# Sums written in place in PSUM, input sums in smaller pieces, and a tile of weights loaded sooner: one core, attention and four experts

## The chip, the cores and the metric

The kernel runs on one core of one Trainium2 chip. Times are microseconds (us) of device time. PE is TensorE, DVE VectorE, ACT ScalarE, POOL GpSimd, SP SyncE.

## The reference

q, k and v (2 batches, 8 heads, 576 positions, 64 columns, float32) are rotated and go through softmax attention. The result, 1152 tokens of 512 columns, goes through four experts, all of them for every token, mixed by weights p:

```python
p = domain_probs / (domain_probs.sum(-1, keepdims=True) + 1e-09)
for e in range(E):                       # E = 4
    h = np.maximum(x @ w1[e], 0.0)       # w1[e]: 512 x 1024
    out += p[:, e:e + 1] * (h @ w2[e])   # w2[e]: 1024 x 512
```

## The kernel before, in words

**High and low halves.** A float32 matrix is held as a high half, rounded to the type that TensorE multiplies (float32r), and a low half, the rest. A product is three matmuls: high by high, high by low, low by high. The split is a copy on ScalarE (`wh`, `hH`, `tH`, ...) and a subtraction on VectorE or GpSimd (`wl`, `hL`, `tL`, ...). Line 142 is the subtraction in the helper `split`; it serves weights, inputs and their sums.

**Chunks.** The tokens go in two chunks. Chunk zero has 512 of batch 0, chunk one the other 640. Attention of batch 0 runs first. Attention of batch 1 runs beside the experts of chunk zero (tiles `ph`, `hH`, `hL`, `po`, lines 557 to 606). Then chunk one runs alone, its four experts one after another: a first layer (products `p`, lines 716 to 718) and a second layer (`po`, lines 796 to 798).

**Chunk one's first layer.** A block of 256 of the 1024 hidden columns is a 2 x 2 block product over two halves of the 512 input columns and two halves of the 640 tokens. It is done with seven block products instead of eight, p1 to p7, from sums of weight blocks (`sf`, split into `sh` and `sl`) and sums of input blocks (class Quarters: `s0` to `s3`, split into `t1H`, `t1L`, `tH`, `tL`). Expert 0 does p1 and p2 of all four blocks first, eight products, then five a block; experts 1 to 3 do seven a block. Each product has 128 partitions x 320 columns and takes one of the eight PSUM banks in turn. VectorE combines the results: `u` = p6 + p1, `v` = p7 + u, `u` = p5 + u; and the four results of a block, `c`, are p5 + v, p2 + p1, p4 + v, p3 + u (line 746, each into an SBUF tile). ScalarE takes relu of `c` as the high half `hH` (line 755), VectorE takes max(c, 0) - hH as the low half `hL` (line 757). The low half is issued one product later, so that it stands behind the next result's add in VectorE's queue.

**Weights.** A tile of 512 KB is loaded by SyncE into one of two raw buffers, copied by ScalarE (`wh`) and subtracted by GpSimd (`wl`), or summed by VectorE first (`sf`). `wts.next()` loads one tile and splits the one before. A raw buffer is free when the last reader of the tile before the last is done; the ring of split tiles has five.

**Order.** The program keeps the order in which it is written. A heap of (time, function) pairs, `plan`, sets that order up to the end of chunk zero: times are positions in the plan, not microseconds, and one step of the experts is one unit. `quarter_step` runs the sums' generators a piece at a time; a `yield` ends a piece. Each engine then runs its own queue in that order, and waits where a semaphore is not yet set.

**The end of chunk zero.** The last pair's attention ends with `tmp` (ScalarE), `xf` (VectorE), 20 matmuls of the tail rows (line 416), a division (line 403), the high half `xH` (line 406) and the low half `xL` (line 409, GpSimd). The last input sums need them. Then VectorE mixes the four `po` of chunk zero's last expert into `acc` (line 606), which frees their banks, and SyncE stores `acc`. In the first layer's class, the bank counter of chunk one starts at 4.

Of the kernel before, what the change touches and what calls it, by code (L numbers as in the profile page):

```python
# [16 lines left out]
AF = mybir.ActivationFunctionType  # L17
# [38 lines left out]
def kernel(  # L56
# [88 lines left out]
    class Pair:  # L145
# [262 lines left out]
        def out_low(self):  # L408
            nc.gpsimd.tensor_tensor(out=self.dst[1], in0=self.xf, in1=f32(self.dst[0]), op=ALU.subtract)

# [112 lines left out]
    class Moe:  # L523
# [18 lines left out]
        def expert(self, e):  # L542
# [24 lines left out]
            for f in range(NF):  # L567
                fb, fi = divmod(f, FB)
                wH, wL = (w[:, fi, :] for w in wts.got[c, e, 1, fb])
                for t in range(n // P):  # L570
                    sH, sL = (x[:, t * P : (t + 1) * P] for x in hh[f])
                    nc.tensor.matmul(po[t], lhsT=sH, rhs=wH, start=(f == 0), stop=False)  # L572
                    nc.tensor.matmul(po[t], lhsT=sH, rhs=wL, start=False, stop=False)  # L573
                    nc.tensor.matmul(po[t], lhsT=sL, rhs=wH, start=False, stop=(f == NF - 1))  # L574
                    if f == NF - 1:
                        self.mix(e, t, po[t])
                if fi == FB - 1:
                    if e == E - 1 and f == NF - 1:
                        wts.load()
                    else:  # L580
                        wts.next()
                yield
# [36 lines left out]
    class Quarters:  # L619
# [25 lines left out]

        def split(self, eng, name, i, j):
            hi, lo = ((y[:, j] for y in self.t1) if i == 0 else (y[:, i - 1, j] for y in self.t))
            split(nc.scalar, eng, self.at[name], hi, lo)

        def first(self, eng, j):  # L650

            self.whole(eng, "s0", j, 0, 1)
            self.whole(eng, "s1", j, 0, 0)
            yield True
            self.less(eng, "s0", ("s1", "s1"))
            self.split(eng, "s1", 0, j)
            yield True

        def second(self, eng, j):

            self.whole(eng, "s2", j, 1, 1)
            self.less(eng, "s2", ("s0", "s0"))
            self.split(eng, "s0", 2, j)
            yield True
            self.less(eng, "s2", ("s2", "s1"))
            self.split(eng, "s2", 1, j)
            yield True
            self.whole(eng, "s3", j, 1, 0)
            self.less(eng, "s3", ("s3", "s2"))
            self.split(eng, "s3", 3, j)  # L670
            yield True
# [9 lines left out]
    class Moe1(Moe):  # L681
# [7 lines left out]
        def __init__(self, ctx, quarters):  # L689
# [6 lines left out]
            ]  # L696
            self.used = 4
            self.x, self.lows = {}, []
# [6 lines left out]
        def product(self, e, i, p):  # L705
# [21 lines left out]
            elif p == "p7":  # L727
                x["v", i] = self.temp("v", e, i)
                self.add(x["v", i], o, x["u", i])
            elif p == "p5":  # L730
                self.hidden(e, 2 * i + 1, 1, o, x["v", i])
                self.add(x["u", i], o, x["u", i])
            elif p == "p2":
# [14 lines left out]
        def hidden(self, e, f, t, o, other):  # L748

            if f not in self.hh:  # L750
                self.hh[f] = [self.h.tile([P, self.n], F32R, tag=f"h{x}{f}", name=f"h{x}1_{e}_{f}") for x in "HL"]
            hi, lo = (x[:, t * TH : (t + 1) * TH] for x in self.hh[f])
            c = self.temp("c", e, f"{f}{t}", 4)
            self.add(c, o, other)
            nc.scalar.activation(out=hi, in_=c, func=AF.Relu)  # L755
            self.lows.append(
                lambda: nc.vector.scalar_tensor_tensor(  # L757
                    out=lo, in0=c, scalar=0.0, in1=f32(hi), op0=ALU.max, op1=ALU.subtract
                )
# [273 lines left out]
    plan.at(end + last - NF + 0.1, start_quarters)  # L1033
    for i in range(7):
        plan.at(end + last - NF + 0.2 + 0.75 * i, quarter_step)
    for i in range(3):
        plan.at(end + last - 1.3 + 0.01 * i, quarter_step)
# [55 lines left out]
```

## Time and profile before

| | us |
|---|---|
| median of 3 runs | 608.73 (608.7 to 613.69) |
| the profiled execution | 611.2, span 609.4 |
| chunk one begins | 373.8 in the span |
| busy TensorE (matmul) | 554.0, 91% |
| busy VectorE, ScalarE, GpSimd | 372.3, 281.2, 332.6 |

The span runs from the first to the last instruction; the time of the profiled execution has 1.8 us around it. The share of a whole run says little here, since chunk one has other limits than attention: waits and stretches of chunk one are what to read.

### The profile page before, as it was taken

How to read it: one execution, taken by the hardware profiler on the slowest of the kernel's cores; microseconds unless marked ns; L12 is line 12 of the kernel's file. 1: busy time of each engine (PE TensorE's matmuls, PEld its weight loads, DVE VectorE, ACT ScalarE, POOL GpSimd, SP SyncE). 2: the span in 40 equal slices, each digit the busy share in tenths (PEclk: the TensorE clock that was granted, in tenths of full speed). 3: DMA queues.
4: the chain of work that ended last, by engine and by line, in shares of the span. 5: the costliest groups of instructions: out<-in, count | busy, mean ns of one | idle time of the engine just before them, and what ended most of it. 6: DMA issues, size and time to landing. Idle time of an engine off the chain costs nothing.

```text
span 609.4 us, 8591 instructions
## 1 busy us (share of the span) xinstructions
PE 554.0 (91%) x3229; PEld 481.6 (79%) x3229; DVE 372.3 (61%) x595; ACT 281.2 (46%) x545; POOL 332.6 (55%) x223
## 2 busy tenths in 40 slices
PE   3788888899999999999999977968998999999896
PEld 2678777778888888888888856957897898789785
DVE  6786898334363435343354335797889788868822
ACT  4677777355444545455355532453243333324310
POOL 7849992257824873485353772364753673466300
PEclk9998999899999999999999998999999999999999
DMA  5053131064124123422332213332232123123102
GB/s 157 7 152 100 36 96 57 1 177 143 69 79 143 57 86 88 130 69 70 96 103 70 70 34 113 94 115 93 71 104 69 38 88 117 35 69 104 35 1 86
DMA packets 42459, 50.67 MB, mean 83 GB/s; under 512 B 7218, under 2 KB 32050, under 8 KB 42418
## 3 DMA queue, kind: packets, MB, share of 16 engines
q1 hardware_dynamic: 41618, 49.38, 27.2%
q10 hardware_dynamic: 800, 0.75, 0.4%
q8 instruction: 25, 0.41, 0.3%
q14 instruction: 16, 0.13, 0.1%
HBM read 43.34 MB, written 2.36 MB: 75 GB/s over the span
## 4 chain that ended last, share of the span: by engine, by line
PE 51%; DVE 17%; POOL 10%; issue 9%; ACT 8%; DMA 5%; SPq 0%; DVEq 0%; POOLq 0%; ACTq 0%
PE sc L282 5%; PE ph L596 4%; POOL wl L142 4%; PE ph L598 4%; PE ph L597 4%; PE po L574 4%; DMA wr<-in_moe_w_dram 4%; PE po L572 4%; PE po L573 4%; PE pp L315 3%; PE po L796 3%; PE po L797 3%; PE po L798 3%; ACT wh L135 3%; POOL sl L142 2%
## 5 line engine op out<-in xcount | busy, mean ns | idle before, releaser
L142 POOL TENSOR_TENSOR wl<-wr,wh 128x1024 fp32r<-128x1024 f32 x64 | 155.4, 2429 | 139.0 <-ACT wh L135 138.9
L135 ACT ACTIVATE wh<-wr 128x1024 fp32r<-128x1024 f32 x64 | 67.4, 1052 | 34.4 <-PE po L574 16.0
L293 DVE TENSOR_REDUCE mx<-sc 128x1 f32<-128x576 f32 x72 | 54.1, 753 | 36.8 <-PE sc L282 36.2
L757 DVE SCALAR_TENSOR_TENSOR hL<-c,hH 128x320 fp32r<-128x320 f32 x64 | 65.7, 1026 | 11.7 <-ACT hH L755 11.6
L142 POOL TENSOR_TENSOR sl<-sf,sh 128x1024 fp32r<-128x1024 f32 x16 | 38.4, 2400 | 62.0 <-ACT sh L135 56.7
L796 PE MATMUL po<-wh,hH 128*128 128x512 f32 x160 | 63.4, 396 | 7.1 <-DVE u L746 4.2
L301 ACT ACTIVATE e<-sc,mx 128x576 f32<-128x576 f32 x72 | 53.2, 740 | 27.7 <-DVE mx L293 27.1
L797 PE MATMUL po<-wl,hH 128*128 128x512 f32 x160 | 62.4, 390 | 0.0
L798 PE MATMUL po<-wh,hL 128*128 128x512 f32 x160 | 62.3, 390 | 0.0
L558 DVE SCALAR_TENSOR_TENSOR hL<-ph,hH 128x512 fp32r<-128x512 f32 x32 | 22.1, 692 | 61.7 <-ACT hH L557 61.7
L755 ACT ACTIVATE hH<-c 128x320 fp32r<-128x320 f32 x64 | 29.8, 468 | 61.8 <-DVE c L746 61.8
L315 PE MATMUL pp<-ident,e 128*128 128x128 f32 x288 | 46.0, 284 | 8.4 <-DVE e L387 5.3
L572 PE MATMUL po<-wh,hH 128*128 128x512 f32 x128 | 52.3, 409 | 0.0
L596 PE MATMUL ph<-xH,wh 128*128 128x512 f32 x128 | 51.5, 402 | 0.0
L336 DVE TENSOR_TENSOR ptL<-pp,ptH 128x512 fp32r<-128x512 f32 x64 | 43.9, 686 | 11.4 <-ACT ptH L332 10.9
L574 PE MATMUL po<-wh,hL 128*128 128x512 f32 x128 | 50.2, 393 | 0.0
L598 PE MATMUL ph<-xH,wl 128*128 128x512 f32 x128 | 50.1, 392 | 0.0
L512 DVE TENSOR_TENSOR sf<-wr 128x256 f32<-128x256 f32 x32 | 38.9, 1255 | 18.3 <-DMA wr<-in_moe_w_dram 18.3
L597 PE MATMUL ph<-xL,wh 128*128 128x512 f32 x128 | 50.0, 391 | 0.0
L573 PE MATMUL po<-wl,hH 128*128 128x512 f32 x128 | 50.0, 391 | 0.0
L332 ACT ACTIVATE ptH<-pp 128x512 fp32r<-128x512 f32 x64 | 38.1, 595 | 25.7 <-PE x L365 17.3
L315 PEld LDWEIGHTS pp<-ident,e 128*128 128x128 f32 x288 | 35.1, 145 | 15.3 <-issue 3.9
(162 smaller groups left out, 1370.6 us busy)
## 6 DMA issues: line engine op xcount, KB each, us to landing
wr<-in_moe_w_dram SPq DMA_DIRECT2D x68, 512.0 KB, 3.5
k2T<-kT SPq DMA_DIRECT2D x14, 288.0 KB, 4.0
rawv<-in_v_dram SPq DMA_DIRECT2D x8, 256.0 KB, 2.9
out_dram<-acc SPq DMA_DIRECT2D x8, 256.0 KB, 2.6
rawk<-in_k_dram SPq DMA_DIRECT2D x7, 256.0 KB, 4.2
rawq<-in_q_dram SPq DMA_DIRECT2D x7, 256.0 KB, 3.2
rawv<-in_v_dram SPq DMA_DIRECT2D x16, 32.0 KB, 2.6
tabs<-in_rope_dram ACTq DMA_DIRECT2D x1, 320.0 KB, 3.3
```

Source lines behind the costliest of these rows:

```text
L135: nc.scalar.activation(out=hi, in_=src, func=AF.Copy)
L142: eng_l.tensor_tensor(out=lo, in0=src, in1=f32(hi), op=ALU.subtract)
L315: nc.tensor.transpose(pp[:, c * P : (c + 1) * P], self.e[u][:, c * P : (c + 1) * P], ident)
L572: nc.tensor.matmul(po[t], lhsT=sH, rhs=wH, start=(f == 0), stop=False)
L573: nc.tensor.matmul(po[t], lhsT=sH, rhs=wL, start=False, stop=False)
L574: nc.tensor.matmul(po[t], lhsT=sL, rhs=wH, start=False, stop=(f == NF - 1))
L596: nc.tensor.matmul(o, lhsT=wH[:, kt], rhs=xh, start=(kt == 0), stop=False)
L597: nc.tensor.matmul(o, lhsT=wH[:, kt], rhs=xl, start=False, stop=False)
L598: nc.tensor.matmul(o, lhsT=wL[:, kt], rhs=xh, start=False, stop=(kt == KT1 - 1))
L796: nc.tensor.matmul(po[t], lhsT=sH, rhs=wH, start=(f == 0), stop=False)
L797: nc.tensor.matmul(po[t], lhsT=sH, rhs=wL, start=False, stop=False)
L798: nc.tensor.matmul(po[t], lhsT=sL, rhs=wH, start=False, stop=(f == NF - 1))
```

## The change

Four edits.

- **Sums in place.** `hidden` adds into the product's own PSUM bank (`o`) rather than into an SBUF tile `c`. Relu and the low half read the bank. For p5 the second sum `u` is therefore made before the add overwrites p5.
- **Input sums in pieces.** Quarters issues sums, high halves and low halves in separate pieces, and more of them are placed in the plan (nine steps 0.6 apart and six at the end, rather than seven 0.75 apart and three). For the last pair of attention the low half `xL` is made by VectorE, not GpSimd.
- **Bank counter.** It starts at 0, not 4. The pool hands out banks as the tags are first asked for: in the built program the first product of chunk one lies in bank 0 before and after, the second in bank 1, and so on.
- **Weights.** In the last expert of chunk zero, the second tile for the weight sums is loaded one step sooner, ahead of the stores of `acc` in SyncE's queue.

```diff
         def out_low(self):
-            nc.gpsimd.tensor_tensor(out=self.dst[1], in0=self.xf, in1=f32(self.dst[0]), op=ALU.subtract)
+            eng = nc.vector if (self.b, self.hp) == (B - 1, NP - 1) else nc.gpsimd
+            eng.tensor_tensor(out=self.dst[1], in0=self.xf, in1=f32(self.dst[0]), op=ALU.subtract)
...
-                if fi == FB - 1:
-                    if e == E - 1 and f == NF - 1:
-                        wts.load()
-                    else:
-                        wts.next()
+                if e == E - 1 and f == NF - 2:
+                    wts.load()
+                elif fi == FB - 1 and (e, f) != (E - 1, NF - 1):
+                    wts.next()
...
         def first(self, eng, j):
             self.whole(eng, "s0", j, 0, 1)
             self.whole(eng, "s1", j, 0, 0)
+            self.less(eng, "s0", ("s1", "s1"))
             yield True
-            self.less(eng, "s0", ("s1", "s1"))
-            self.split(eng, "s1", 0, j)
+            self.high("s1", 0, j)
             yield True
+            self.low(eng, "s1", 0, j)
         def second(self, eng, j):
             self.whole(eng, "s2", j, 1, 1)
             self.less(eng, "s2", ("s0", "s0"))
-            self.split(eng, "s0", 2, j)
+            self.less(eng, "s2", ("s2", "s1"))
             yield True
-            self.less(eng, "s2", ("s2", "s1"))
-            self.split(eng, "s2", 1, j)
+            self.high("s0", 2, j)
+            self.high("s2", 1, j)
             yield True
             self.whole(eng, "s3", j, 1, 0)
             self.less(eng, "s3", ("s3", "s2"))
-            self.split(eng, "s3", 3, j)
+            self.low(eng, "s0", 2, j)
+            self.low(eng, "s2", 1, j)
+            yield True
+            self.high("s3", 3, j)
+            yield True
+            self.low(eng, "s3", 3, j)
             yield True
...
-            self.used = 4
+            self.used = 0
...
             elif p == "p5":
+                self.add(x["u", i], o, x["u", i])
                 self.hidden(e, 2 * i + 1, 1, o, x["v", i])
-                self.add(x["u", i], o, x["u", i])
...
-            c = self.temp("c", e, f"{f}{t}", 4)
-            self.add(c, o, other)
-            nc.scalar.activation(out=hi, in_=c, func=AF.Relu)
+            self.add(o, o, other)
+            nc.scalar.activation(out=hi, in_=o, func=AF.Relu)
             self.lows.append(
                 lambda: nc.vector.scalar_tensor_tensor(
-                    out=lo, in0=c, scalar=0.0, in1=f32(hi), op0=ALU.max, op1=ALU.subtract
+                    out=lo, in0=o, scalar=0.0, in1=f32(hi), op0=ALU.max, op1=ALU.subtract
...
-    for i in range(7):
-        plan.at(end + last - NF + 0.2 + 0.75 * i, quarter_step)
-    for i in range(3):
+    for i in range(9):
+        plan.at(end + last - NF + 0.2 + 0.6 * i, quarter_step)
+    for i in range(6):
         plan.at(end + last - 1.3 + 0.01 * i, quarter_step)
```

ScalarE's queue in the last steps of chunk zero, before, from the copy of the tail's transposed exponentials (`at`) to the high halves of the last input sums:

```order
L351 ACTIVATE at_3_8_3865<-pp_3_8_3860 128x512
L135 ACTIVATE t1H<-s_3837 128x320
L372 ACTIVATE tmp_3_3_3872<-x_112 64x256
L135 ACTIVATE wh_0_0_3_3889<-wr_0_0_3_3818 128x1024
L425 ACTIVATE xH_74<-x_112 128x64
L406 ACTIVATE xH_74<-xf_3_3537 128x512
```

and now:

```order
L351 ACTIVATE at_3_8_3861<-pp_3_8_3856 128x512
L372 ACTIVATE tmp_3_3_3870<-x_112 64x256
L651 ACTIVATE t1H<-s_3866 128x320
L135 ACTIVATE wh_0_0_3_3888<-wr_0_0_3_3821 128x1024
L426 ACTIVATE xH_74<-x_112 128x64
L406 ACTIVATE xH_74<-xf_3_3537 128x512
```

`tmp`, which the last tile of attention needs, and `t1H`, the high half of an input sum that GpSimd makes, have changed places. Two high halves `tH` have moved ahead of the `tmp` before this one, too.

VectorE's queue from the last division of attention to the first mixing of chunk zero's output (`acc`), before:

```order
L403 TENSOR_TENSOR xf_3_3537<-xf_3_3537,pr_3_3903 128x512
L429 TENSOR_TENSOR xL_76<-x_112,xH_74 128x64
L639 TENSOR_TENSOR s_3925<-xH_74,xL_76 128x320
L644 TENSOR_TENSOR s_3835<-s_3925,s_3835 128x320
L142 TENSOR_TENSOR tL<-s_3835,tH 128x320
L644 TENSOR_TENSOR s_3925<-s_3925,s_3837 128x320
L142 TENSOR_TENSOR tL<-s_3925,tH 128x320
L639 TENSOR_TENSOR s_3933<-xH_74,xL_76 128x320
L644 TENSOR_TENSOR s_3933<-s_3933,s_3925 128x320
L142 TENSOR_TENSOR tL<-s_3933,tH 128x320
L606 SCALAR_TENSOR_TENSOR acc_0_1511<-po_3_0_3673,probs,acc_0_1511 128x512
```

and now:

```order
L403 TENSOR_TENSOR xf_3_3537<-xf_3_3537,pr_3_3902 128x512
L430 TENSOR_TENSOR xL_76<-x_112,xH_74 128x64
L410 TENSOR_TENSOR xL_76<-xf_3_3537,xH_74 128x512
L639 TENSOR_TENSOR s_3927<-xH_74,xL_76 128x320
L644 TENSOR_TENSOR s_3864<-s_3927,s_3864 128x320
L644 TENSOR_TENSOR s_3927<-s_3927,s_3866 128x320
L639 TENSOR_TENSOR s_3933<-xH_74,xL_76 128x320
L644 TENSOR_TENSOR s_3933<-s_3933,s_3927 128x320
L655 TENSOR_TENSOR tL<-s_3864,tH 128x320
L655 TENSOR_TENSOR tL<-s_3927,tH 128x320
L655 TENSOR_TENSOR tL<-s_3933,tH 128x320
L606 SCALAR_TENSOR_TENSOR acc_0_1511<-po_3_0_3673,probs,acc_0_1511 128x512
```

The 512-column `xL` is new in this queue, and the three low halves, each of which needs a high half from ScalarE, stand together behind the five sums.

VectorE's queue in the second block of expert 1's first layer, before:

```order
L746 TENSOR_TENSOR u_1_4643<-p_1_4636,p_1_1_4633 128x320
L746 TENSOR_TENSOR v_1_4652<-p_1_4645,u_1_4643 128x320
L746 TENSOR_TENSOR c_31_4663<-p_1_4654,v_1_4652 128x320
L746 TENSOR_TENSOR u_1_4643<-p_1_4654,u_1_4643 128x320
L746 TENSOR_TENSOR c_20_4676<-p_1_4667,p_1_1_4633 128x320
L757 SCALAR_TENSOR_TENSOR hL_1_3_4662<-c_31_4663,hH_1_3_4661 128x320
L746 TENSOR_TENSOR c_30_4687<-p_1_4680,v_1_4652 128x320
L757 SCALAR_TENSOR_TENSOR hL_1_2_4675<-c_20_4676,hH_1_2_4674 128x320
```

and now:

```order
L759 TENSOR_TENSOR u_1_4623<-p_1_4616,p_1_1_4613 128x320
L759 TENSOR_TENSOR v_1_4632<-p_1_4625,u_1_4623 128x320
L759 TENSOR_TENSOR u_1_4623<-p_1_4634,u_1_4623 128x320
L759 TENSOR_TENSOR p_1_4634<-p_1_4634,v_1_4632 128x320
L759 TENSOR_TENSOR p_1_4646<-p_1_4646,p_1_1_4613 128x320
L769 SCALAR_TENSOR_TENSOR hL_1_3_4643<-p_1_4634,hH_1_3_4642 128x320
L759 TENSOR_TENSOR p_1_4658<-p_1_4658,v_1_4632 128x320
L769 SCALAR_TENSOR_TENSOR hL_1_2_4654<-p_1_4646,hH_1_2_4653 128x320
```

The number of operations is the same. `p` stands where `c` stood, as output of the add and as first input of `hL`, and `u` goes ahead of the add for p5.

## Rows read from the trace of the kernel before

**Rows 1.** Waits of TensorE, 373 to 609: total us, times, longest us.

```profile
PE p L716 <- DVE acc L606: 4.3, 2, 3.5
PE po L796 <- DVE u L746: 4.2, 3, 1.4
PE p L716 <- DVE u L746: 3.4, 4, 1.1
PE p L716 <- DVE v L746: 3.1, 2, 1.9
PE po L796 <- DVE v L746: 1.6, 1, 1.6
PE po L796 <- DVE c L746: 1.3, 1, 1.3
PE p L716 <- DVE c L746: 0.5, 1, 0.5
```

**Rows 2.** Timeline, expert 1: start, us, engine, line, operation [idle before <-releaser].

```profile
452.27 0.48 DVE L746 TENSOR_TENSOR u<-p,p 128x320 f32<-128x320 f32 x1
...
457.07 2.40 POOL L142 TENSOR_TENSOR wl<-wr,wh 128x1024 fp32r<-128x1024 f32 x1 [5.07 <-ACT wh L135]
457.39 2.43 DVE L757 SCALAR_TENSOR_TENSOR hL<-c,hH 128x320 fp32r<-128x320 f32 x1 [0.65 <-ACT hH L755]
459.74 0.48 DVE L746 TENSOR_TENSOR u<-p,p 128x320 f32<-128x320 f32 x1
```

**Rows 3.** Tiles c, hL: min/median/max ns, first and last start.

```profile
L755 ACT ACTIVATE hH<-c x64: 450/472/493, 385.8 to 582.0; 128x320 fp32r<-128x320 f32 x64
L757 DVE SCALAR_TENSOR_TENSOR hL<-c,hH x64: 474/482/2448, 386.3 to 582.5; 128x320 fp32r<-128x320 f32 x64
L746 DVE TENSOR_TENSOR c<-p,v x32: 477/488/493, 391.8 to 580.6; 128x320 f32<-128x320 f32 x32
...
L558 DVE SCALAR_TENSOR_TENSOR hL<-ph,hH x32: 682/692/694, 117.8 to 335.7; 128x512 fp32r<-128x512 f32 x32
```

**Rows 4.** Timeline, chunk zero: a low half from PSUM under a GpSimd operation.

```profile
118.83 2.40 POOL L142 TENSOR_TENSOR wl<-wr,wh 128x1024 fp32r<-128x1024 f32 x1 [2.57 <-ACT wh L135]
120.58 0.69 DVE L558 SCALAR_TENSOR_TENSOR hL<-ph,hH 128x512 fp32r<-128x512 f32 x1 [2.05 <-ACT hH L557]
```

**Rows 5.** Timeline, TensorE in two first layers, expert 0 and expert 1.

```profile
376.21 0.47 PE L717 MATMUL p<-xL,wh 128*128 128x320 f32 x1
...
381.81 0.34 PE L717 MATMUL p<-xL,wh 128*128 128x320 f32 x1
...
457.31 0.31 PE L716 MATMUL p<-xH,wh 128*128 128x320 f32 x1
...
458.19 0.31 PE L716 MATMUL p<-tH,sh 128*128 128x320 f32 x1
```

**Rows 6.** Timeline, the end of chunk zero, engine by engine.

```profile
361.09 0.47 ACT L135 ACTIVATE t1H<-s 128x320 fp32r<-128x320 f32 x1 [3.09 <-POOL s L644]
361.59 0.38 ACT L372 ACTIVATE tmp<-x 64x256 f32<-64x256 f32 x1
362.47 1.80 PE L416 MATMUL x<-at,rawv 128*64 128x64 f32 x20 [2.52 <-DVE xf L376]
366.32 1.29 POOL L409 TENSOR_TENSOR xL<-xf,xH 128x512 fp32r<-128x512 f32 x1 [0.97 <-ACT xH L406]
367.65 0.49 DVE L639 TENSOR_TENSOR s<-xH,xL 128x320 f32<-128x320 f32 x1 [1.93 <-POOL xL L409]
373.00 2.72 DVE L606 SCALAR_TENSOR_TENSOR acc<-po,probs,acc 128x512 f32<-128x512 f32 x4
```

**Rows 7.** Stretches: PE, PEld, DVE, ACT, POOL busy (x), PEclk, DMA share, GB/s.

```profile
360.00:364.00 4.00, 1.53 (x19) 1.33 (x20) 0.42 (x1) 1.80 (x3) 2.85 (x4) 1.00 0.00 0
376.00:378.00 2.00, 2.00 (x8) 2.00 (x9) 1.15 (x4) 0.78 (x1) 0.00 (x0) 0.50 0.99 301
```

**Rows 8.** Timeline, ScalarE in expert 0's first layer.

```profile
405.97 1.06 ACT L135 ACTIVATE wh<-wr 128x1024 fp32r<-128x1024 f32 x1 [2.56 <-DMA wr<-in_moe_w_dram]
```

More of the change, by code (lines that the diff above doesn't have):

```diff
@@ L644, in less, with halves, high, low @@
             eng.tensor_tensor(out=self.at[b[0]], in0=self.at[a], in1=self.at[b[1]], op=ALU.subtract)
-        def split(self, eng, name, i, j):
-            hi, lo = ((y[:, j] for y in self.t1) if i == 0 else (y[:, i - 1, j] for y in self.t))
-            split(nc.scalar, eng, self.at[name], hi, lo)
+        def halves(self, i, j):
+            return ((y[:, j] for y in self.t1) if i == 0 else (y[:, i - 1, j] for y in self.t))
+        def high(self, name, i, j):
+            hi, _ = self.halves(i, j)
+            nc.scalar.activation(out=hi, in_=self.at[name], func=AF.Copy)
+        def low(self, eng, name, i, j):
+            hi, lo = self.halves(i, j)
+            eng.tensor_tensor(out=lo, in0=self.at[name], in1=f32(hi), op=ALU.subtract)
         def first(self, eng, j):
```

## The prediction

> **What bounds the kernel now.** I read the waits of TensorE first, from the start of chunk one to the end [rows 1]. Every one of them ends with VectorE: 4.3 us at the change of chunks (two waits, behind the mixing of chunk zero) and 4.2 + 3.4 + 3.1 + 1.6 + 1.3 + 0.5 = 14.1 us behind `u`, `v` and `c`, the sums of first-layer results. So in chunk one TensorE is the bound except in the first layers, where VectorE is late. 6.5 us of the 14.1 lie in expert 0 (all of `v` and `c`: 3.1 + 1.6 + 1.3 + 0.5), 7.6 us in experts 1 to 3 (all of `u`).
>
> Why VectorE is late shows in one block of expert 1 [rows 2]. From one first `u` to the next, 452.27 to 459.74, VectorE needs 7.47 us. In it the last lower half `hL` takes 2.43 us, and it ends when GpSimd's `wl`, started just before it, ends (457.07 + 2.40 = 459.47). The median `hL` takes 0.482 us, the longest 2.448 [rows 3]. The same form with its first input in PSUM, `hL<-ph` of chunk zero, is 0.694 us at most in 32 cases, on 512 columns rather than 320 [rows 3]; one of them lies wholly inside a `wl` and takes 0.69 [rows 4]. So the operand's place decides: with two SBUF inputs VectorE waits until GpSimd's operation is over, with one it does not.
>
> TensorE needs less per block: six matmuls, one product, from 457.31 to 458.19 [rows 5], 0.88 us; a block of experts 1 to 3 has seven products, 6.2 us. The 1.3 us by which VectorE's 7.47 is longer is what the waits collect.
>
> The change of chunks is a chain of short steps [rows 6]. `t1H` stands in ScalarE's queue until 361.09 for a GpSimd sum; `tmp` behind it starts at 361.59; TensorE waits 2.52 us for it, until 362.47. Then GpSimd's `xL` (366.32, 1.29 us), then VectorE from 367.65, sums and lower halves in turn with ScalarE, and the mixing `acc` at 373.00, after which chunk one starts. Behind this TensorE's clock is at its lower level: 0.50 granted, 1.2 GHz, where it was 1.00 before [rows 7]; 21 matmul steps from 376.21 to 381.81 take 0.267 us each [rows 5] against 0.147.
>
> **The change, part by part.** The sums are made against the profiled execution, 611.2 us with a span of 609.4; the median of the runs shown is 608.73. I take the gain off both alike.
>
> 1. *Sums in place in PSUM.* `c` is gone; add, relu and `hL` work on the bank. `hL` now has one SBUF input, like `hL<-ph`. Block of VectorE: 7.47 - (459.74 - 457.39 = 2.35) + 0.48 = 5.60 us [rows 2, 3], under TensorE's 6.2. The trace has no VectorE operation that writes PSUM. The nearest row is today's `c`, same shape and inputs, 0.488 us [rows 3]; if reading and writing one bank took turns it would be twice that. Four adds at 0.98 make the block 7.6 us, the old pace; I take 0.49, because the inputs already come from PSUM and the output is the only thing that moves. That the add is cheaper than 0.48 is the other end, and would give nothing, since TensorE is then the bound.
>  What is held longer: a bank is now released by `hL`, not by the add, so by relu (0.47, [rows 3]) and one or two VectorE steps later, about 1.5 us. TensorE comes back to a bank eight products later, 8 x 0.88 = 7.0 us. That covers it while VectorE keeps pace. In experts 1 to 3 I take all of the 7.6 us off; the least is 4 us, if half of the waits come back as bank waits.
>  In expert 0 there are five products a block (4.4 us) and the weights' sums on VectorE besides, so the cover is thin. Relu now releases banks, and it stands in ScalarE's queue behind `wh`, which waits for weights there: 2.56 us at 405.97 [rows 8]. I charge that wait in full: 6.5 - 2.6 = 3.9 us off; the ends are 0 and 6.5.
>  The swap of `u` and the add for p5 is needed by the overwriting; it moves a 0.49 us step ahead of another on the same engine: nothing.
>
> 2. *Other banks first (`used = 0`).* Costed at nothing, because I think it does nothing: the pool hands out banks in the order in which tags are first asked for, and the first tag asked for gets bank 0 whatever its number is; in the built program the first product lies in bank 0 before and after. If it did act, the first products would not wait for `acc` at all, for 2 us more, the sum of the two short waits that item 3 leaves.
>
> 3. *Input sums in pieces.* In the new order `tmp` is ahead of `t1H` on ScalarE. The 2.52 us wait goes; the work that hides `tmp` is the second layer of chunk zero's last expert, which runs until 359.95 (362.47 - 2.52). Against it, two more `tH` stand ahead of the `tmp` before, each behind a GpSimd sum of 320 columns; from GpSimd's 1.29 us for 512 columns [rows 6] one is about 0.8 us (an estimate), and I take most of one, 0.6 us, as delay of the last tile of attention. Net 1.9. `xL` on VectorE: about 0.69 instead of 1.29 us, by the 512-column row [rows 3, 6], 0.6 off, and one change of engine less, 0.1. On VectorE, from 367.65 to 373.00, eight operations stand with a ScalarE step between sum and lower half three times; now all sums come first. Eight at 0.488 and one wait left of 0.3 make 4.2 instead of 5.35: 1.2 off. Together 1.9 + 0.7 + 1.2 = 3.8 us. Ends: 2.0 (the wait for `tmp` comes back elsewhere) and 5.0.
>  `xL` now has two SBUF inputs on VectorE, and GpSimd's last lower half `t1L` may run at that moment; by the 2.43 us row [rows 2] it would then wait for it, up to 0.8 us. I leave this out of the sum, since `t1L` is queued behind nothing that is late; the range holds it.
>  The Trainium skill, page "SBUF — State Buffer", section "Who interferes with whom", says that a VectorE instruction with two SBUF inputs contends with a GpSimd instruction that reads SBUF, for the whole of it, and one with a single SBUF input does not. It speaks for the new `hL` and against `xL`, the sums and the lower halves moved onto VectorE: by it, with `t1L` in the way, item 3 would be 3.0 and the time 591.7. The rows agree as far as they go: 2.43 against 0.69 us under a `wl`.
>
> 4. *Clock.* Today's fall to 0.50 comes behind a TensorE wait of 3.5 us and a second of 0.8 [rows 1, 7]. Item 3 leaves two of about 1 us. Around the 2.52 us wait at 360 the granted clock stayed at 1.00 [rows 7]. So I take the fall as gone: 21 x (0.267 - 0.147) = 2.5 us; the other end is 0.
>
> 5. *Weights sooner.* The load of the second new tile leaves SyncE ahead of the four output stores rather than behind. It waits only for the raw buffer, which the last `wl` of chunk zero frees before GpSimd's `xL` at 366.32, nearly 7 us before the stores can follow `acc` at 373.00 [rows 6]. No engine waits in SyncE's queue. Its gain is that VectorE's second weight sum is not late; that is inside the 3.9 of expert 0.
>
> Sum: 3.8 + 2.5 + 3.9 + 7.6 = 17.8 us. 611.2 - 17.8 = 593.4 against the profiled execution; **608.7 - 17.8 = 590.9** against the median. With the best ends 5.0 + 2.5 + 6.5 + 7.6 = 21.6 the time is 587.1; with the worst of all four at once, 2.0 + 0 + 0 + 4 = 6.0, it is 602.7.
>
> **Rivals.**
> - *The wait moves to ScalarE.* Banks come free behind relu, relu stands behind `wh`, `wh` waits for weights: each first layer keeps half its waits, and expert 0 all of them. For it speaks the 2.56 us wait [rows 8]; against it that in experts 1 to 3 one split falls on 6.2 us of products. 3.8 + 2.5 + 0 + 3.8 = 10.1, so 598.6.
> - *`hL` stays blocked.* If the relu's result or the output, both still in SBUF, were what GpSimd blocks, VectorE keeps 7.47 us a block, and banks are held 0.8 us longer (two VectorE steps) at the end of four first layers. 6.3 - 3.2 = 3.1 gained: 605.6. Against it: 32 rows of the same form, none above 0.694 [rows 3, 4].
> - *The in-place add is dear, and the kernel slower.* Place: the four adds of a block. From the length at which the block passes 7.47 + 6.3/16 = 7.86 us, so an add of 0.488 + (7.86 - 5.60)/4 = 1.05 us, nothing is gained. At three times 0.488 = 1.46 us the block is 9.5 and the time 608.7 + 16 x 2.0 - 6.3 = 634. Nothing in the profile shows it; nothing shows a VectorE write to PSUM either.
> - *The bank edit does act*: 588.9, against the banks of the built program.
>
> **How the numbers follow.** Forecast, 590.9 with its own range 586 to 596: 0.64. Wait on ScalarE: 0.20. `hL` still blocked: 0.07. Dear add: 0.04. Bank edit: 0.05. The range 586 to 601 holds the forecast, the bank edit and the ScalarE case with most of their spread (not all four worst ends at once); it leaves out the blocked `hL`, the dear add and the tails. A change of 1% (6.1 us) is about what a measurement of this kernel can tell from none. Faster by over 1%: 0.64 + 0.20 + 0.05 = 0.89; within 1%: 0.07; slower: 0.04.
>
> **What would show it.** Right: no `hL` of chunk one above 0.6 us; the in-place add near 0.49; no TensorE wait on VectorE in the first layers of experts 1 to 3; the first product of chunk one still waiting for `acc`, near 369 to 370 us; granted clock 1.00 behind it; what is left of waits in expert 0, on `hL` behind a ScalarE `wh`. Wrong: adds above 0.9 us, `hL` as long as a `wl`, or bank waits in every first layer.

## The result and the profile after

| | us |
|---|---|
| before, median of 4 runs beside it | 610.37 (608.70 to 613.69) |
| changed kernel, median of 4 runs | **587.89** (586.93 to 588.82) |
| ratio | 0.9625, 95% interval 0.9574 to 0.9677 |
| its profiled execution | 588.56, span 586.8 |
| busy VectorE | 341.3 (372.3 before) |

The forecast was 590.9, with a range of 586 to 601; 587.9 lies in it. The gain is 22.5 us against the runs beside it (20.8 against the 608.73 from which the forecast was made) where the sum said 17.8. The mechanism held; one term was too small, one failed, and one that had no price of its own turned out to be worth over 3 us.

Waits of TensorE in the changed kernel, 340 to the end, the counterpart of [rows 1]: total us, times, longest us.

```profile
PE po L808 <- DVE hL L769: 2.6, 2, 1.8
PE p L729 <- DVE acc L606: 2.5, 2, 1.7
PE pp L315 <- DVE e L387: 1.8, 1, 1.8
PE x L365 <- DVE ptX L348: 0.2, 1, 0.2
```

The 14.1 us behind `u`, `v` and `c` are gone. What is left is 2.5 us behind `acc` at the change of chunks and 2.6 us behind `hL` in expert 0. Experts 1 to 3 have no wait.

Why, the tiles' durations show, for `hH` and `hL` as in [rows 3]: min/median/max ns.

```profile
L767 ACT ACTIVATE hH<-p x64: 415/438/442, 376.5 to 555.5; 128x320 fp32r<-128x320 f32 x64
L769 DVE SCALAR_TENSOR_TENSOR hL<-p,hH x64: 477/486/494, 377.2 to 556.0; 128x320 fp32r<-128x320 f32 x64
```

The longest of 64 `hL` is 494 ns, where it was 2448. One of them under a `wl`, and the in-place add (`p<-p,v`) of the block before it, in the timeline of the changed kernel in expert 1 (GpSimd first, then VectorE):

```profile
442.56 2.42 POOL L142 TENSOR_TENSOR wl<-wr,wh 128x1024 fp32r<-128x1024 f32 x1 [3.24 <-ACT wh L135]
```

```profile
437.59 0.48 DVE L759 TENSOR_TENSOR u<-p,p 128x320 f32<-128x320 f32 x1
...
439.17 0.49 DVE L759 TENSOR_TENSOR p<-p,v 128x320 f32<-128x320 f32 x1
...
442.84 0.49 DVE L769 SCALAR_TENSOR_TENSOR hL<-p,hH 128x320 fp32r<-128x320 f32 x1 [0.59 <-ACT hH L767]
443.25 0.48 DVE L759 TENSOR_TENSOR u<-p,p 128x320 f32<-128x320 f32 x1
```

`hL` at 442.84 starts 0.28 us after the `wl` and takes 0.49; the one in [rows 2], in the same position, took 2.43. From one first `u` to the next it is 443.25 - 437.59 = 5.66 us, forecast 5.60. The adds that write PSUM take 0.49.

The change of chunks, as in [rows 6], engine by engine in the changed kernel:

```profile
356.85 0.38 ACT L372 ACTIVATE tmp<-x 64x256 f32<-64x256 f32 x1
...
360.22 2.39 POOL L142 TENSOR_TENSOR wl<-wr,wh 128x1024 fp32r<-128x1024 f32 x1 [2.30 <-ACT wh L135]
362.58 0.87 POOL L655 TENSOR_TENSOR t1L<-s,t1H 128x320 fp32r<-128x320 f32 x1
...
362.12 0.63 ACT L406 ACTIVATE xH<-xf 128x512 fp32r<-128x512 f32 x1 [1.08 <-DVE xf L403]
...
362.79 1.21 DVE L410 TENSOR_TENSOR xL<-xf,xH 128x512 fp32r<-128x512 f32 x1 [0.56 <-ACT xH L406]
...
367.76 2.72 DVE L606 SCALAR_TENSOR_TENSOR acc<-po,probs,acc 128x512 f32<-128x512 f32 x4
...
370.39 0.75 DVE L513 TENSOR_TENSOR sf<-wr 128x256 f32<-128x256 f32 x2
```

`tmp` no longer stands behind `t1H`, and the 2.52 us wait for it is gone. `xL` takes 1.21 us, because GpSimd's `t1L` began just before it; `t1L` itself stood behind a `wl`.

The clock behind the change of chunks, as in [rows 7] (the granted clock is the column ahead of the last two):

```profile
370.00:372.00 2.00, 1.47 (x5) 1.48 (x6) 1.97 (x6) 0.03 (x1) 0.00 (x0) 0.61 1.04 375
372.00:374.00 2.00, 2.00 (x9) 2.00 (x9) 1.36 (x4) 1.53 (x2) 0.90 (x1) 0.53 0.53 145
374.00:376.00 2.00, 2.00 (x16) 2.00 (x15) 0.08 (x1) 1.86 (x5) 2.00 (x2) 1.00 0.88 256
```

It still falls, to 0.53, for 11 slow matmul steps instead of 21.

**Stretches.** The span of one execution differs from that of another by several us before the change begins: the first `hH` of chunk zero starts at 117.2 us in one kernel's profile and at 111.6 in another's, though the instructions up to there are the same. So I compare stretches from that point on. In the table each entry is a difference of two start times in one profiled execution: from that `hH` to the first product of chunk one ("change"), the four experts from first product to first product, and in all up to the last matmul. For before the starts are 117.2, 373.80, 438.31 (expert 1) and 604.38 (last matmul); for the changed kernel 116.4, 368.55, 426.40 and 581.75.

| kernel | change | expert 0 | experts 1 to 3 | in all | slow steps |
|---|---|---|---|---|---|
| before | 256.60 | 64.51 | 166.07 | 487.18 | 21 |
| **changed** | 252.19 | 57.85 | 155.35 | 465.39 | 11 |
| in_place | 256.14 | 61.14 | 155.35 | 472.63 | 22 |
| pieces | 252.53 | 63.99 | 166.08 | 482.60 | 10 |
| load | 256.06 | 60.60 | 166.25 | 482.91 | 9 |
| banks | 257.48 | 63.86 | 166.51 | 487.85 | 8 |
| no_read | 257.86 | 65.89 | 155.35 | 479.10 | 21 |
| xl_pool | 252.76 | 58.57 | 155.35 | 466.68 | 21 |
| split_later | 252.04 | 54.99 | 157.41 | 464.44 | 13 |
| upper_banks | 250.50 | 59.13 | 155.35 | 464.98 | 0 |
| all_three | 250.41 | 55.47 | 157.36 | 463.24 | 1 |
| third_raw | 252.38 | 54.85 | 155.35 | 462.58 | 11 |
| all_four | 250.36 | 54.07 | 155.35 | 459.78 | 0 |

"Slow steps" are the matmul steps of about 0.267 us in the first 20 us of chunk one, counted to within one. The kernels below "changed" are the experiments.

How far these stretches vary by chance can be read from the table. before, in_place, load, banks and no_read give TensorE, VectorE, ScalarE and GpSimd the same instructions up to the first product, and their "change" runs from 256.06 to 257.86. before and banks are the same program, and their expert 0 takes 64.51 and 63.86. Experts 1 to 3 are far steadier: 155.35 in seven kernels, 166.07 to 166.51 in four. One of the ten runs of banks took 3016.82 us, for a reason that nothing here shows, and is left out of its ratio.

### The profile page after: what moved, and what is told of

It is laid out like the page before. It is cut to its first block, busy times and chain, and to the rows that moved or that the text cites. A ratio compares the mean times of both kernels' runs of the same rounds, so it can differ in the third digit from the quotient of the medians.

```text
span 586.8 us, 8596 instructions
## 1 busy us (share of the span) xinstructions
PE 548.2 (93%) x3229; PEld 480.3 (82%) x3229; DVE 341.3 (58%) x596; ACT 279.4 (48%) x545; POOL 331.0 (56%) x222
## 4 chain that ended last, share of the span: by engine, by line
PE 73%; DVE 11%; ACT 6%; POOL 5%; DMA 2%; issue 2%; SPq 0%; ACTq 0%; DVEq 0%; POOLq 0%
PE po L808 6%; PE po L809 6%; PE po L810 6%; PE p L729 5%; PE p L730 5%; PE p L731 5%; PE sc L282 4%; PE ph L596 4%; PE ph L598 4%; PE ph L597 4%; PE po L575 4%; PE po L573 4%; PE po L574 4%; PE pp L315 3%; PE x L417 2%; ACT e L301 2%
## 5 line engine op out<-in xcount | busy, mean ns | idle before, releaser
L767 ACT ACTIVATE hH<-p 128x320 fp32r<-128x320 f32 x64 | 27.4, 434 | 43.3 <-DVE p L759 43.0
L135 ACT ACTIVATE sh<-sf 128x1024 fp32r<-128x1024 f32 x16 | 17.0, 1060 | 59.1 <-DVE sf L513 59.1
```

Of the source, the lines that this page charges most:

```text
L135: nc.scalar.activation(out=hi, in_=src, func=AF.Copy)
```

## Experiments: the parts alone

The four edits, each alone on the kernel before, ran beside 25 runs of before (median 609.54).

**in_place**

```diff
-            c = self.temp("c", e, f"{f}{t}", 4)
-            self.add(c, o, other)
-            nc.scalar.activation(out=hi, in_=c, func=AF.Relu)
+            self.add(o, o, other)
+            nc.scalar.activation(out=hi, in_=o, func=AF.Relu)
```

(and `hL` reads `o`; `u` ahead of the add for p5)

> Kernel before with the sums in place in PSUM alone (and p5's second sum ahead of its first). Theory: hL with one SBUF input is not held up by GpSimd, so every hL of chunk one is under 0.6 us, the in-place adds take about 0.49, and TensorE has no wait in the first layers of experts 1 to 3. Those three experts become as short as in the changed kernel, 10.7 us less in all than before; expert 0 loses 3 to 5 us of its 64.5; the change of chunks stays where it was (first product of chunk one at 373.8, clock low behind it). About 596, 14 less than before. Rival 1, hL stays blocked by its SBUF output or by relu's result: within 3 of before. Rival 2, the listed waits of 7.6 us are all there was to gain in experts 1 to 3 and the other 3 us came from another edit (pieces or load): about 599.

Measured: 594.39, ratio 0.9764 (0.9709 to 0.9819): faster than before, whether by 2% stays open. Experts 1 to 3 take 155.35 us, to the hundredth what the changed kernel takes. The waits that are left (same columns as above):

```profile
PE p L716 <- DVE acc L606: 4.3, 2, 3.5
PE po L795 <- DVE hL L756: 2.6, 1, 2.6
PE x L416 <- DVE xf L376: 2.6, 1, 2.6
PE pp L315 <- DVE e L387: 1.6, 1, 1.6
PE p L716 <- DVE hL L756: 0.4, 1, 0.4
```

The whole 10.7 us come from this edit; rival 2 falls. The change of chunks keeps its waits of 4.3 and 2.6. Expert 0 falls by 64.51 - 61.14 = 3.4.

**pieces**

```diff
+            eng = nc.vector if (self.b, self.hp) == (B - 1, NP - 1) else nc.gpsimd
...
-    for i in range(7):
+    for i in range(9):
...
-    for i in range(3):
+    for i in range(6):
```

(and class Quarters as in the change)

> Kernel before with the input sums in pieces alone (their places in the plan, and the last xL on VectorE). Theory: the wait of TensorE for tmp (2.52 us) is gone, xL takes about 1.2 us on VectorE because GpSimd's t1L runs beside it, chunk one's first product starts 5 us earlier in the span of which 1.5 come from a stretch ahead of the last plan steps, and the clock still falls, for about ten slow matmuls rather than 21. hL stays at 2.4 us under a wl, so experts 1 to 3 stay as before. 5 to 6.5 less than before: about 604. Rival: the gain at the change of chunks needs the earlier load of weights too, and the first product starts no earlier than 372: within 2 of before.

Measured: 605.36, ratio 0.9934 (0.9905 to 0.9964), 4.2 less where 5 to 6.5 were expected. The change of chunks is 4.1 us shorter, without any help from the load; experts 1 to 3 stay at 166.08. A clock fall with 10 slow steps instead of 21 leaves expert 0 only 0.5 us shorter.

**load**

```diff
-                if fi == FB - 1:
-                    if e == E - 1 and f == NF - 1:
-                        wts.load()
-                    else:
-                        wts.next()
+                if e == E - 1 and f == NF - 2:
+                    wts.load()
+                elif fi == FB - 1 and (e, f) != (E - 1, NF - 1):
+                    wts.next()
```

> Kernel before with the one load of weights a step sooner alone. Theory: the second tile for the weight sums lands a few us sooner, but expert 0 is held by hL under wl and by later tiles: 0 to 1.5 less than before, all of it in expert 0. Rival, the load is what shortened expert 0 (6.7 us in the changed kernel) : 3 or more less.

Measured: 605.89, ratio 0.9949 (0.9916 to 0.9983), 3.65 less. Expert 0 falls by 64.51 - 60.60 = 3.9, nearly all of it in its first layer (33.61 to 29.82). A part of this can be the clock, which fell for 9 slow steps instead of 21: against banks, the same program as before with 8 slow steps, expert 0 is 63.86 - 60.60 = 3.3 shorter. Of the two, the rival is right. VectorE's sums of weights (start, us, engine, line, operation [idle before <-releaser]), first before, then with the load sooner:

```profile
375.64 0.75 DVE L512 TENSOR_TENSOR sf<-wr 128x256 f32<-128x256 f32 x2
...
381.89 0.76 DVE L512 TENSOR_TENSOR sf<-wr 128x256 f32<-128x256 f32 x2 [4.71 <-DMA wr<-in_moe_w_dram]
```

```profile
369.46 0.75 DVE L512 TENSOR_TENSOR sf<-wr 128x256 f32<-128x256 f32 x2
...
370.92 0.75 DVE L512 TENSOR_TENSOR sf<-wr 128x256 f32<-128x256 f32 x2
```

Before, VectorE stands 4.71 us on the load of the second tile, and every sum of first-layer results is queued behind it; with the load sooner the second sum follows the first.

**banks**

```diff
-            self.used = 4
+            self.used = 0
```

> Kernel before with the bank counter at 0 instead of 4 alone. Theory: the pool hands out banks by first request, the built program is the same on every engine, so the time is that of before (ratio 1.00 within its interval). Rival, the edit acts: 2 or more less, the first product of chunk one ahead of the mixing of chunk zero.

Measured: 610.54, ratio 1.0015 (0.9987 to 1.0043): nothing, as the built program says.

Against before, in the table's last sums, the three that act give 14.55 + 4.58 + 4.27 = 23.4 us alone and 21.8 together. In expert 0 they overlap: 3.4 + 0.5 + 3.9 = 7.8 alone, 6.7 together.

## Experiments: the cause, and what is left

**no_read** tests the cause from GpSimd's side: `c` and `hL` are as before.

```diff
-            split(nc.scalar, nc.gpsimd, raw, wh, wl)
+            if c and e:
+                nc.scalar.activation(out=wh, in_=raw, func=AF.Copy)
+                nc.gpsimd.memset(f32(wl), 0.0)
+            else:
+                split(nc.scalar, nc.gpsimd, raw, wh, wl)
```

(the same for `sl`)

> Kernel before, in which GpSimd fills the low halves wl and sl of the weights of experts 1 to 3 of chunk one with zeros instead of subtracting: the low halves of those weights are left out of the result. GpSimd then works without reading SBUF, and hL still has two SBUF inputs. Theory, what held hL was GpSimd reading SBUF beside it: every hL of experts 1 to 3 takes 0.48, TensorE has no wait on u there, and the three experts take 155 to 156 instead of 166.1, as with the sums in place. Rival, an hL with two SBUF inputs is held by any GpSimd operation beside it, or by its place behind relu: hL stays long where the filling runs, and the experts stay above 160.

Measured: experts 1 to 3 take 155.35 us, again the same to the hundredth (the one run took 599.4, with experts 1 to 3 without low halves of their weights). The tile `hL`, 430 to 600, min/median/max ns:

```profile
L765 DVE SCALAR_TENSOR_TENSOR hL<-c,hH x48: 481/482/495, 442.2 to 566.8; 128x320 fp32r<-128x320 f32 x48
```

The fill takes 0.96 us where the subtraction took 2.40, so the question is whether any `hL` still stands beside one. 13 of the 48 do, and take 0.481 to 0.483. Here is one (GpSimd, then VectorE):

```profile
448.96 0.96 POOL L502 MEMSET wl<- 128x1024 f32 x1 [5.20 <-PE p L726]
```

```profile
449.29 0.48 DVE L765 SCALAR_TENSOR_TENSOR hL<-c,hH 128x320 fp32r<-128x320 f32 x1
```

So two SBUF inputs are not slow in themselves, and a GpSimd that only writes holds nothing up; together with in_place it is shown from both sides that `hL` waited for GpSimd's reading of SBUF. The Trainium skill, page "SBUF — State Buffer", section "Who interferes with whom", says this too: the contention is with a GpSimd instruction that reads SBUF, not with one that only writes it. The run agrees, 0.495 us at most against 2.448.

**xl_pool**

```diff
-            eng = nc.vector if (self.b, self.hp) == (B - 1, NP - 1) else nc.gpsimd
-            eng.tensor_tensor(out=self.dst[1], ...)
+            nc.gpsimd.tensor_tensor(out=self.dst[1], ...)
```

> Changed kernel with the last xL back on GpSimd. In the changed kernel it stood 1.21 us on VectorE with GpSimd's t1L beside it (0.87 from 362.58). Theory: on GpSimd it starts behind t1L, at about the same 363.4, and takes 1.29: xL lands 0.7 us later, and the stretch from the first hH of chunk zero to the first product of chunk one, 252.2 in the changed kernel, becomes 252.9. Too little for the times of whole runs to tell; the stretch is what is read. Rival 1, the order of the low halves is all that counts: the stretch stays within 0.2 of 252.2. Rival 2, VectorE's five sums then run beside nothing and xL's move was a loss: the stretch is shorter.

Measured: 589.19, ratio to before 0.9663 (0.9621 to 0.9705); the stretch is 252.76, 0.57 longer. That alone is within what chance does to this stretch. A shorter one is steadier: from the last `xH` to the first product it is 8.17 to 8.19 in the five kernels with the old order, 6.43 in the changed kernel (362.12 to 368.55) and 7.09 here (362.00 to 369.09), 0.66 longer. So the size is the forecast one, and the reason is another. GpSimd, then VectorE, in that kernel:

```profile
362.70 1.29 POOL L409 TENSOR_TENSOR xL<-xf,xH 128x512 fp32r<-128x512 f32 x1 [0.22 <-ACT xH L406]
363.95 0.88 POOL L654 TENSOR_TENSOR t1L<-s,t1H 128x320 fp32r<-128x320 f32 x1
```

```profile
364.03 1.15 DVE L638 TENSOR_TENSOR s<-xH,xL 128x320 f32<-128x320 f32 x1 [1.93 <-POOL xL L409]
...
366.15 0.49 DVE L638 TENSOR_TENSOR s<-xH,xL 128x320 f32<-128x320 f32 x1
```

`xL` stands ahead of `t1L` there, and then `t1L` holds up VectorE's first sum, 1.15 us instead of 0.49. Moving `xL` moved the collision from that sum to `xL` itself.

**split_later** goes at the 2.6 us that are left in expert 0. In the changed kernel ScalarE, VectorE and TensorE stand there in a row:

```profile
395.85 1.06 ACT L135 ACTIVATE wh<-wr 128x1024 fp32r<-128x1024 f32 x1 [4.54 <-DMA wr<-in_moe_w_dram]
...
397.27 0.49 DVE L769 SCALAR_TENSOR_TENSOR hL<-p,hH 128x320 fp32r<-128x320 f32 x1 [3.63 <-ACT hH L767]
...
397.81 0.50 PE L808 MATMUL po<-wh,hH 128*128 128x512 f32 x1 [1.76 <-DVE hL L769]
```

```diff
-                if e == 0 and i < 2:
+                if e == 0 and i < 1:
                     wts.next()
...
-                if fi == FB - 1:
+                if fi == FB - 1 or (e, f) == (0, 0):
                     wts.next()
```

> Changed kernel, in which expert 0's first layer splits one tile of weights fewer, and its second layer one more, behind its first hidden block. In the changed kernel ScalarE's wh waits 4.54 us for that tile's load, and relu and hL queue behind it, so that the second layer's TensorE waits 2.6 us in two places. Theory: with the split behind them, hL is ready and these waits are gone: expert 0 falls from 57.9 to about 55.2. Rival 1: the wait was one for weights; the later split makes the second layer wait for wh instead, and expert 0 stays within 0.5. Rival 2: the ring of weights falls a tile behind, and expert 1 gets the waits.

Measured: 587.21, ratio to before 0.9621 (0.9575 to 0.9667), no different from the changed kernel. Expert 0 is 2.9 us shorter, as the theory has it, and expert 1 is 2.1 longer (53.92 instead of 51.86): the gain is given back there, as rival 2 has it, though not by the ring. VectorE, then TensorE, around the change from expert 0 to expert 1 in that kernel:

```profile
421.25 3.82 DVE L513 TENSOR_TENSOR sf<-wr 128x256 f32<-128x256 f32 x2 [2.58 <-DMA wr<-in_moe_w_dram]
...
425.78 3.38 DVE L604 TENSOR_SCALAR acc<-po,probs 128x512 f32<-128x512 f32 x5
```

```profile
426.58 0.42 PE L729 MATMUL p<-t1H,sh 128*128 128x320 f32 x1 [0.70 <-DVE acc L604]
```

VectorE waits for a load, its sums, which have two SBUF inputs, then stand under an `sl` and a `wl` of GpSimd (3.82 us where free they take 0.75), and the mixing behind them frees the banks that expert 1 wants. Counted from the first `hH` of chunk zero, the sums start at 305.2 here and at 305.6 in the changed kernel, and the mixing at 309.7 in both: a wait removed ahead of them is given back behind. That the loads set this pace is argued here; third_raw tests it.

**upper_banks** makes the bank edit act.

```diff
+            for i in range(8):
+                self.pp.tile([P, 512], F32, tag=f"m{i}", name=f"m{i}")
-            self.used = 0
+            self.used = 4
```

> Changed kernel, in which the bank edit really acts: the eight tags are asked for in order first, and the counter starts at 4, so that the first four products take the banks that attention had, and the next four those of chunk zero's output. Theory A, the edit's promise: the first product does not wait for the mixing, the stretch from the first hH of chunk zero to it falls from 252.2 to about 250.3, TensorE's clock has no reason to fall, and chunk one's end comes 2 to 3 us earlier. Theory B, the gain is given back: the sums of weights stand on VectorE behind the mixing, and ScalarE's copies of the p1 products behind their high halves, so that p6 of the first block waits 1 to 2 us and the end comes 0 to 1 us earlier. I hold B the likelier, 0.6.

Measured: 586.52, ratio to before 0.9619 (0.9572 to 0.9665). The first product comes 252.19 - 250.50 = 1.7 us sooner, the clock does not fall at all (1.00 from 366 to 384), and expert 0 is 1.3 us longer: theory B. The wait that it names is there:

```profile
376.00 0.41 PE L731 MATMUL p<-tH,sh 128*128 128x320 f32 x1 [1.04 <-ACT p L738]
```

**all_three**

```diff
                 for i in range(nb):
+                    self.product(e, i, "p1")
+                wts.split()
+                wts.next()
+                for i in range(nb):
+                    self.product(e, i, "p2")
```

(in place of split, next and then p1 and p2; with the edits of split_later and upper_banks)

> Changed kernel with the later split and the banks of the two runs beside it, and with the four p1 products of expert 0 issued ahead of the first sum of weights, so that ScalarE's copies of them stand ahead of its high half. Theory: the waits of the second layer (2.6 us) go, the first product comes 2 us earlier, and of these 2 us about one is kept, since the low half of the first weight sum on GpSimd is then the last thing that p6 needs. About 3.5 less than the changed kernel, 584. Rival: what ends expert 0's first layer is the chain mixing, sums, high half, low half alone, and nothing of the 2 us is kept: 585.3.

Measured: 584.92, ratio to before 0.9601 (0.9562 to 0.9641); in all 463.24, 2.2 less than the changed kernel, where 3.5 was expected. The 2 us of expert 1 are there again (53.87).

**third_raw**

```diff
-            raw = wpool.tile([P, FB * DM], F32, tag="raw", ..., bufs=NRAW)
+            third = hasattr(self, "pool") and self.loaded % 3 == 2
+            pool, bufs = (self.pool, 1) if third else (wpool, NRAW)
+            raw = pool.tile([P, FB * DM], F32, tag="raw", ..., bufs=bufs)
...
+                wts.load()
                 wts.split()
                 wts.next()
```

> Changed kernel with a third raw buffer for weights from chunk one on (it fits where the tiles c were), and one load more in flight. In the changed kernel VectorE's second sum in the second layer of expert 0 waits 3.04 us for a load, and the mixing of expert 0 stands behind it; with the later split this became expert 1's wait. Theory, in expert 0 the supply of weights is the bound: with a load more in flight ScalarE's wh and VectorE's sf no longer wait for loads in the second layer, and expert 0 falls from 57.9 to about 55. Rival 1: the loads are already back to back, so that one more in flight lands no sooner; expert 0 within 0.5. Rival 2: the additional load takes time from the stores of chunk zero's output or from its own predecessor, and the first layer of expert 0 gets longer by 1 to 2.

Measured: 583.62, ratio to before 0.9589 (0.9559 to 0.9618). Expert 0 takes 54.85, 3.0 less, and nothing is given back in expert 1. The wait on `hL` is gone from the list:

```profile
PE p L731 <- DVE acc L608: 2.5, 2, 1.7
PE pp L315 <- DVE e L387: 1.8, 1, 1.8
PE x L365 <- DVE ptX L348: 0.2, 1, 0.2
```

So the loads were not back to back; they waited for one of two raw buffers. The waits of SyncE's queue in the changed kernel agree: from 366 to 426 its loads wait 31.6 us, in seven waits, for GpSimd's `wl`, which reads a raw buffer. The space for the third is what `c` had.

**all_four** is all_three with third_raw.

> The three edits together (later split, other banks, p1 products first) and the third raw buffer. Theory: with the supply of weights a load ahead, the 2 us that expert 1 got back in the three edits together are gone, and the gain of 2.4 in expert 0 and of 1.8 at the change of chunks stays: first hH of chunk zero to the end 461, where the changed kernel has 465.4, and a median of about 583. Rival, GpSimd is the bound of the splits (2.4 us a tile) and no sooner load helps: the 2 us stay, 463.2 as with the three edits.

Measured: **581.99** (580.45 to 584.26), ratio to before 0.9563 (0.9536 to 0.9591). In all it takes 459.78, 5.6 us less than the changed kernel, and its slowest run is under the fastest of the changed kernel (586.93); the two ran beside different runs of before. What it leaves from the change of chunks on is one wait of 1.5 us, in the first layer of expert 0:

```profile
374.60 0.42 PE L735 MATMUL p<-tH,sl 128*128 128x320 f32 x1 [1.50 <-POOL sl L142]
```

The chain behind the mixing (sum on VectorE, high half on ScalarE, low half on GpSimd) is now the last to end there. To put the first sum ahead of the mixing was not tried; in the program its tiles come from a pool that is opened with chunk one.

## Why the prediction was right, and where it was wrong

By stretches the gain is 21.8 us, 4.0 above the sum: 3.1 of it in experts 1 to 3, 0.6 at the change of chunks, 0.3 in expert 0.

- **Item 1, experts 1 to 3: right mechanism, term too small.** 7.6 forecast, 10.7 measured, all by in_place. The step that failed is taking listed waits for lost time. In expert 1 of before, three waits are listed with 0.26 + 1.04 + 1.41 = 2.71 us; from matmul start to matmul start, over the usual pitch, the same three places lose 3.52, and a fourth that the list does not have (at 469.0) loses 0.19. The list counts idle only from the modelled end of the last matmul, and the matmul behind a wait is followed later than usual. Here is the middle one, with its 1.04:

```profile
458.92 0.31 PE L718 MATMUL p<-tH,sl 128*128 128x320 f32 x1
460.27 0.41 PE L716 MATMUL p<-tH,sh 128*128 128x320 f32 x1 [1.04 <-DVE u L746]
460.52 0.31 PE L717 MATMUL p<-tL,sh 128*128 128x320 f32 x1
```

 460.27 - 458.92 = 1.35 and 460.52 - 460.27 = 0.25 stand where two pitches of 0.147 would: 1.31 lost, not 1.04. The sum could have gone by stretches: four blocks of seven products at 0.88 us are 24.6 us for a first layer, and 24.64 is what each of them now takes, while expert 1's took 26.46 before.
 The reading of [rows 2] is off by a little: `hL` ends at 457.39 + 2.43 = 459.82, 0.35 us behind the `wl` and not with it. It is the waiting that ends with the `wl`; no term of the sum changes.
- **Item 1, expert 0: near.** 3.9 forecast with 2.6 of waits left; alone the edit gives 3.4 and leaves 2.6 + 0.4, and in the changed kernel 2.6 stand behind `wh`, as said.
- **Item 2: right.** Nothing (1.0015). That it would have given 2 us if it acted was wrong: it does give 1.7 at the start, and 1.3 are lost again.
- **Item 3: right in size**, 3.8 forecast, 4.4 in the changed kernel and 4.1 alone, but in part by luck, since its terms miss in both directions. Counted from the first `hH` of chunk zero, the last `xH` starts 2.7 us sooner (1.9 forecast; this part holds the chance of the clock in chunk zero). From there to VectorE's first sum it takes 1.97 instead of 2.03 us, 0.06 less (0.7 forecast). From that sum to the mixing it takes 3.67 instead of 5.35, 1.7 less (1.2 forecast). The term that failed is the second: `xL` ran into `t1L` after all, 1.21 instead of 0.69 us. I had set that aside with "`t1L` is queued behind nothing that is late"; in the new order it is queued behind a `wl` that waits 2.30 us for ScalarE's `wh`. The rule that the prediction cites from the Trainium skill, page "SBUF — State Buffer", section "Who interferes with whom", described this collision. The trace agrees (1.21 us), but the 3.0 for item 3 did not come, since the other two terms gave more. Nor was the move a loss: on GpSimd the collision falls on VectorE's next sum (xl_pool, 0.66 us worse).
- **Item 4: wrong.** "I take the fall as gone": it came all the same. The premise, that the clock stays at 1.00 around a wait of 2.52 us, was read from one execution. banks is the same program, and behind the same wait its granted clock was 0.50 (358.53 to 362.53), and the 20 matmuls of the tail took 2.97 us where [rows 6] have 1.80:

```profile
358.54 2.97 PE L416 MATMUL x<-at,rawv 128*64 128x64 f32 x20 [2.52 <-DVE xf L376]
```

 The price was wrong, too. pieces has 11 slow steps fewer than before, by the sum 1.3 us, and its expert 0 is 0.5 shorter; banks has 13 fewer, by the sum 1.6, and its expert 0 is 0.65 shorter. So a slow step cost about 0.05 us there, not 0.12. That VectorE and ScalarE are the bound behind the change of chunks, and hide the rest, is argued and not shown.
- **Item 5: wrong as an item.** "Inside the 3.9 of expert 0": alone it gives 3.3 to 3.9 us. I saw that VectorE's second sum of weights is late without it, and gave that no price of its own. The row with the price is VectorE's (4.71 us on a DMA), and it is not among the rows that I worked from; TensorE's list shows the same time only under the names `v` and `c`. The forecast for expert 0, 2.5 + 3.9 = 6.4, met 6.7 by luck: the 2.5 of the clock, of which at most a part came, and the missing price of the load cancel.
- **Rivals.** The wait that moves to ScalarE happened in expert 0 alone. A blocked `hL`, a dear add (it takes 0.49) and an acting bank edit did not happen.

## What to carry to other kernels

When TensorE waits for a VectorE result, read what VectorE itself waited for, several instructions back: here a GpSimd operation that reads SBUF and a load, both under the names of sums. Here one of two SBUF inputs was put into PSUM, and that wait went. Price a wait from matmul start to matmul start against the undisturbed pitch, and compare executions by stretches from a common event, the shorter the better: from the last `xH` on, kernels of the same order agree to 0.02 us, and over the 250 us before it to about 2.

## What the runs showed of the hardware

- An add on VectorE that reads and writes the same PSUM bank takes 0.49 us for 128 x 320, as much as one into SBUF ([rows 3]: 0.488).
- A VectorE instruction with two SBUF inputs is held until the GpSimd instruction that reads SBUF beside it ends: in [rows 2] `hL` ends 0.35 us behind the `wl` and takes 2.43 us in all, where undisturbed it takes 0.48. The same instruction beside a GpSimd fill is not held (482 ns median).
- The granted clock falls at different places in executions of the same instructions. Two stretches of before, then of load; up to 350 us the two kernels have the same instructions:

```profile
44.00:52.00 8.00, 6.85 (x50) 6.43 (x51) 3.73 (x8) 3.51 (x9) 7.67 (x8) 0.79 0.17 44
104.00:112.00 8.00, 5.52 (x32) 4.89 (x32) 5.48 (x10) 3.63 (x10) 2.93 (x3) 0.80 0.00 0
```

```profile
44.00:52.00 8.00, 5.99 (x56) 5.46 (x56) 4.93 (x9) 4.46 (x12) 7.67 (x8) 1.00 0.16 44
104.00:112.00 8.00, 7.64 (x54) 6.10 (x52) 2.86 (x8) 2.16 (x5) 1.29 (x1) 1.00 0.00 0
```

 0.79 and 0.80 in the one, 1.00 in the other. This goes with a part of the 5.6 us between the two at the first `hH` of chunk zero; how large a part stays open. Behind the wait of 2.5 us ahead of the tail's matmuls the clock fell in two of the five executions that have it (banks and no_read). A forecast should treat a single clock fall as a chance, not as a term.
